# Attention and a maxout feed-forward net in one kernel: the last 64 queries of both heads as 64x64 matmul tiles

## The chip, the cores and the metric

The kernel runs on one core of a Trainium2 chip. The metric is the device time of one launch in microseconds; the profile's span, from the first to the last instruction, is a little shorter.

## The reference

Attention over 8 batches of 12 heads, 448 tokens and a head dimension of 64, with one extra term in the softmax's denominator, is followed by a three-way maxout feed-forward net over all 3584 tokens. Cut to its core:

```python
scores = scale * np.matmul(q, k.transpose(0, 1, 3, 2))
m = np.max(scores, axis=-1, keepdims=True)
e = np.exp(scores - m)
attn = e / (np.sum(e, axis=-1, keepdims=True) + np.exp(-m) + 1e-09)
attn_out = np.matmul(attn, v)
x = attn_out.transpose(0, 2, 1, 3).reshape(B * S, H * D)      # 3584 x 768
h = np.maximum(np.maximum(x @ w1, x @ w2), x @ w3)            # 768 x 768 each
out = h @ w_out                                               # 768 x 768, float32
```

## The kernel before

**Groups and pairs.** The 96 heads are worked in 24 groups (`NI`) of four heads, three groups to a batch; a group has two pairs (`pr`) of two heads (`hh`). Inputs are cast to float16 by the loading DMAs. K and Q are brought to head-dimension-first form, for the later groups by DMA transposes on SP's queue (`transpose_dma`), and GpSimd copies shifted halves of Q (`shift_q`).

**Scores.** `scores` computes transposed scores, so keys lie on partitions. The 448 keys of a head are seven blocks of 64, and a 128-partition tile holds two of them. Three such tiles hold six blocks of one head (`X1`, `X3`, `X2`); the seventh blocks of both heads of a pair share one (`TL`). A unit is two such tiles side by side in the two banks of one PSUM tile `stp`, made by four 64x64 matmuls, each in its own quarter of the array; ScalarE's exponential (L320) writes it to `e`.

**Weighted sums.** `av_tail` and `av_main` multiply `e` by V into a two-bank PSUM tile `avp`, one bank per head. V has a 65th column of constants, whose sum is the denominator. The 448 queries are cut into windows `w` of 128, so the fourth (`w` = 3) has only 64 real queries, and its other 64 weight columns are whatever lies next to them in `e`. `av_tail` covers the shared seventh blocks: for each window and head two 64x64x65 matmuls (L340), four to a window. `av_main` covers the other six blocks: for each head and window three 128x128x65 matmuls (L357). VectorE then makes the reciprocal of the denominators in `rb` (L367, L370) and writes the scaled sums to `xn` (L373).

**To the feed-forward net.** From group 6 on, a DMA transpose on SP's queue (`x_transpose_dma`, L423) brings `xn` to `xT`. The net's work for a batch is a list of pieces: 18 up pieces of six 128x128x448 matmuls (L440, PSUM tile `p_i`; VectorE takes the maximum into `hT`, L449 and L451), and 6 or 8 out pieces of six matmuls of 384 columns (L464, `op_ps`; VectorE scales them to `o_sb`, L471; SP's queue stores them, L481).

**PSUM.** The pool `ps_s` has three two-bank buffers, used in turn by `stp` and `avp`; `ps_b` has two one-bank buffers, used in turn by `p_i` and `op_ps`.

**Order.** It is written out by hand. From group 3 on each group has three visits, numbered `n` = 3i + vi. A visit issues the scores of two, two and three units, then in the first two visits `av` for one pair of the group before, and then pieces: `share(n)` gives the visit its part of the columns of work left, and `fill` pops pieces until a running `credit` is used up. The batch that is next is added by `add_batch` at the visits in `adds`. After the last visit come both `av` of group 23, its `x_transpose_dma`, what pieces are left, and the last batch.

Of the kernel before, what the change touches and what calls it, by code (L numbers as in the profile page):

```python
# [10 lines left out]
FP32 = mybir.dt.float32  # L11
FP16 = mybir.dt.float16
AF = mybir.ActivationFunctionType
ALU = mybir.AluOpType
ts = bass.ts

MMDT = FP16
LAMBDA = 256.0
# [3 lines left out]
def kernel(  # L22
# [11 lines left out]
    nc = tc.nc  # L34

    B, H, S, D = q.shape
# [5 lines left out]
    NP = GH // 2  # L42
    NG = H // GH
    NI = B * NG
    P = 128
    HP = 64
# [3 lines left out]
    D1 = D + 1  # L50
    XW = 512
    scale = 1.0 / math.sqrt(D)
# [3 lines left out]
    PE_QK = 7  # L56
    NF = 3
    PE_X = 2
    NEB = 2
    NV = 3  # L60

    cpool = ctx.enter_context(tc.tile_pool(name="const", bufs=1))
    att_pool = ctx.enter_context(tc.tile_pool(name="att", bufs=3))
    small = ctx.enter_context(tc.tile_pool(name="small", bufs=3))
    xn_pool = ctx.enter_context(tc.tile_pool(name="xn", bufs=3))
    xt_pool = ctx.enter_context(tc.tile_pool(name="xt", bufs=3))
    ht_pool = ctx.enter_context(tc.tile_pool(name="ht", bufs=2))
    out_pool = ctx.enter_context(tc.tile_pool(name="outp", bufs=6))
# [64 lines left out]
    first = {}  # L133
    for nm, src, eng in (("k", k, nc.sync), ("q", q, nc.scalar)):
# [7 lines left out]
            name=nc.get_next_instruction_name(),  # L142
# [13 lines left out]

    e_buf = [cpool.tile([P, NB * S + HP], MMDT, name=f"e{j}") for j in range(NEB)]
    v_buf = [cpool.tile([P, GH, 3, D + 2], MMDT, name=f"vx{j}") for j in range(NV)]
    vt_buf = [cpool.tile([P, NP, D + 2], MMDT, name=f"vt{j}") for j in range(NV)]
    for j in range(NV):  # L160
        nc.vector.memset(v_buf[j][:, :, :, D : D + 2], 1.0 / LAMBDA)
        nc.vector.memset(vt_buf[j][:, :, D : D + 2], 1.0 / LAMBDA)
    for j in range(NEB):
        nc.vector.memset(e_buf[j][:, NB * S : NB * S + HP], 0.0)
        blk = e_buf[j][:, 0 : NB * S].rearrange("p (n s) -> p n s", s=2 * S)
        nc.vector.memset(blk[:, :, NO : NO + HP], 0.0)

    def warm(n, cols=512):
        ps = ps_b.tile([128, 512], FP32, tag="b", name="warm")
# [104 lines left out]
    X1, X2, X3, TL = (0, 4), (2, 6), (1, 5), (3, 3)  # L274
# [9 lines left out]
    where = {(pr, hh, x): n for n, (pr, hh, x) in enumerate(blocks)}  # L284
# [37 lines left out]
    def e_col(n, w):  # L322

        return n * S + ((192, 320, 0, 128) if n % 2 == 0 else (0, 128, 256, 384))[w]

    xT = {}
    xn = {}
    avs = {}

    def av_tail(i, ej, pr, ws=(0, 1, 2, 3)):  # L330

        eF, vt = e_buf[ej], vt_buf[i % NV]
        ps = ps_s.tile([128, 2, 512], FP32, tag="s", name="avp")
        avs[i, pr] = ps
        n = where[pr, None, TL]
        for j, w in enumerate(ws):
            for hh in range(2):
                for half in range(2):
                    o = e_col(n, w) + half * HP
                    nc.tensor.matmul(  # L340
                        out=ps[half * HP : half * HP + HP, hh, j * D1 : (j + 1) * D1],
                        lhsT=eF[hh * HP : hh * HP + HP, o : o + HP],
                        rhs=vt[hh * HP : hh * HP + HP, pr, 0:D1],
                        start=(j == 0),
                        stop=False,
                        skip_group_check=True,
                    )

    def av_main(i, ej, pr, ws=(0, 1, 2, 3)):
        eF, vx = e_buf[ej], v_buf[i % NV]  # L350
        ps = avs.pop((i, pr))
        nw = len(ws)
        for hh in range(2):
            for j, w in enumerate(ws):
                for c, x in enumerate((X1, X3, X2)):
                    o = e_col(where[pr, hh, x], w)
                    nc.tensor.matmul(  # L357
                        out=ps[:, hh, j * D1 : (j + 1) * D1],
                        lhsT=eF[:, o : o + 128],
                        rhs=vx[:, 2 * pr + hh, (x[0]), 0:D1],  # L360
                        start=False,
                        stop=(c == 2),
                        skip_group_check=True,
                    )
        acc = ps[:, :, 0 : nw * D1].rearrange("p h (j d) -> p h j d", d=D1)
        rb = small.tile([P, 2, 4], FP32, tag="rb", name="rb")
        nc.vector.tensor_scalar(  # L367
            out=rb[:, :, 0:nw], in0=acc[:, :, :, D], scalar1=1.0 / LAMBDA, scalar2=None, op0=ALU.add
        )
        nc.vector.reciprocal(out=rb[:, :, 0:nw], in_=rb[:, :, 0:nw])  # L370
        if i not in xn:
            xn[i] = xn_pool.tile([P, NP, 4, 2, D], MMDT, tag="xn", name="xn")
        nc.vector.tensor_tensor(  # L373
            out=xn[i][:, pr, ws[0] : ws[0] + nw].rearrange("p j h d -> p h j d"),
            in0=acc[:, :, :, 0:D],
            in1=rb[:, :, 0:nw].unsqueeze(3).to_broadcast([P, 2, nw, D]),
            op=ALU.mult,
        )

    def prep_v(i, eng):  # L380
        t = raw[i]["v"]
        vx, vt = v_buf[i % NV], vt_buf[i % NV]
        eng.tensor_copy(out=vx[:, :, :, 0:D], in_=t[:, :, 1:4, :])  # L383
        t2 = t.rearrange("p (r h) t d -> p r h t d", r=NP)
        eng.tensor_copy(out=vt[0:HP, :, 0:D], in_=t2[0:HP, :, 0, 4, :])
        eng.tensor_copy(out=vt[HP:P, :, 0:D], in_=t2[HP:P, :, 1, 0, :])
# [34 lines left out]
    def x_transpose_dma(i):  # L421
        b, g = groups[i]
        nc.sync.dma_start_transpose(  # L423
            out=xt_tile(b)[:, 2 * g : 2 * g + 2, :].rearrange("p a (j s) -> p (a j) s", s=128),
            in_=xn[i].rearrange("p a j h d -> p (a j h d)"),
        )
# [61 lines left out]
    pieces = []  # L488
# [20 lines left out]
    credit = [0.0]  # L509

    def fill(cols):
        credit[0] += cols
        while pieces and credit[0] > 0:
            f, a, w = pieces.pop(0)
            f(*a)
            credit[0] -= w
        if not pieces:
            credit[0] = min(credit[0], 0.0)

    def left():  # L520
        return sum(w for _, _, w in pieces)

# [3 lines left out]
    STEP = 2 * NDC * (NO + 6)  # L526

    def av(i, ej, pr, part):
        av_tail(i, ej, pr, PW[part])
        av_main(i, ej, pr, PW[part])  # L530

# [6 lines left out]
    def attend(part, g, *steps):  # L538

        ej = (g + (part == "E") * NG) % NEB  # L540
        for st in steps:
# [3 lines left out]
            else:  # L545
                pg, pr = st[1:]
                av(pg, pg % NEB, pr, "O")

# [52 lines left out]
    visits = ((0, 1), (2, 3), (4, 5, 6))  # L601
    adds = {3 * (3 * b + 4) + (b >= PE_X): b for b in range(1, B - 1)}

    AVC = 2200

    def share(n):


        nxt = min([a for a in adds if a > n], default=3 * NI + 2)
        rest = range(n, nxt)  # L610
        sums = [AVC if m % 3 < 2 and m < 3 * NI else 0 for m in rest]
        return max(0, (left() + sum(sums)) / len(rest) - sums[0])
# [7 lines left out]
    for i in range(3, NI):  # L620
        ej, pj = (i + 1) % NEB, i % NEB
        first = i == 3
        if PE_QK <= i + 2 < NI:
            transpose_dma(i + 2)
        if first:
            load_v(i + 2)
        for vi, units in enumerate(visits):
            n = 3 * i + vi
            scores(i, ej, units)
            if i == 4 and vi == 0:  # L630
                prep_v(i, DV)
            if vi < 2:
                av(i - 1, pj, vi, "E" if first else "EO")
            if vi == 1 and i > 3 * PE_X:
                x_transpose_dma(i - 1)
            if n in adds:
                add_batch(adds[n])
            per = STEP if first and vi < 2 else share(n)
            if vi == 0 and first:
                x_transpose_pe(1, "E")  # L640
            if vi == 2 and first:
                x_transpose_pe(i - 1, "E")
                fill(per / 2)
                prep_v(i, DV)
                for w, cols in ((0, (0, NE)), (1, (0, NE)), (2, (NE, NO)), (2, (0, NE))):
                    add_up(0, *cols, [(w, f) for f in (0, 2, 4)])
                add_out(0)
                per = share(n)
            if vi == 2 and 3 < i <= 3 * PE_X:
                x_transpose_all(i - 1)  # L650
            if first:
                fill(per)
                per = 0
            if i + 1 < PE_QK and vi < 2:
                transpose_once(i + 1, "qk"[vi], (AC, DV)[vi])
            fill(per)
        if i + 1 < PE_QK:
            shift_q(i + 1, nc.gpsimd)
        if first:
            load_qk(i + 3)  # L660
        if i < 5:
            load_more(i + 3, i + 4)
        if 5 <= i + 1 < NI:
            prep_v(i + 1, nc.gpsimd)
        if PE_QK <= i + 2 < NI:
            shift_q(i + 2, nc.gpsimd)
        if i >= 5:
            load_more(i + 3, i + 4)

    av(NI - 1, NI % NEB, 0, "EO")  # L670
    av(NI - 1, NI % NEB, 1, "EO")
    x_transpose_dma(NI - 1)
    fill(float("inf"))
    add_batch(B - 1)
# [31 lines left out]
```

The softmax here doesn't subtract the row's maximum and nothing guards it: scores larger than these inputs give would overflow.

## Time and profile before

| | |
|---|---|
| median of 8 runs | 341.21 us (340.9 to 342.44) |
| the profiled execution: time / span | 341.24 us / 339.5 us |
| PE busy | 329.8 us, 97% |
| DVE busy | 189.3 us, 56% |
| ACT busy | 151.0 us, 44% |
| POOL busy | 146.7 us, 43% |
| mean granted TensorE clock | 0.996 |

The busy shares come from one profiled execution. A busy PE counts overlapping matmuls once, so matmuls are best priced by the distance between their starts. A group's row gives the line, the engine, the operation, what is written and read, the shapes, the count, the busy time, the mean of one, and the idle time of the engine before it with what ended it. A timeline's row gives the start, the time from the first start to the last end, the engine and what ran, merged over equal neighbours.

### The profile page before, as it was taken

How to read it: one execution, taken by the hardware profiler on the slowest of the kernel's cores; microseconds unless marked ns; L12 is line 12 of the kernel's file. 1: busy time of each engine (PE TensorE's matmuls, PEld its weight loads, DVE VectorE, ACT ScalarE, POOL GpSimd, SP SyncE). 2: the span in 40 equal slices, each digit the busy share in tenths (PEclk: the TensorE clock that was granted, in tenths of full speed). 3: DMA queues.
4: the chain of work that ended last, by engine and by line, in shares of the span. 5: the costliest groups of instructions: out<-in, count | busy, mean ns of one | idle time of the engine just before them, and what ended most of it. 6: DMA issues, size and time to landing. Idle time of an engine off the chain costs nothing.

```text
span 339.5 us, 9812 instructions
## 1 busy us (share of the span) xinstructions
PE 329.8 (97%) x4172; PEld 199.5 (59%) x4172; DVE 189.3 (56%) x410; ACT 151.0 (44%) x181; POOL 146.7 (43%) x260
## 2 busy tenths in 40 slices
PE   7899999999999999999999999999999999999994
PEld 4668788855555655555555655555555655555552
DVE  4556665565546555555545555546456556465552
ACT  3868856654554545453543445463543454200000
POOL 8686677971836077154547071936252000000000
PEclk9999999999999999999999999999999999999998
DMA  8999999699996997979996999999970440133006
GB/s 148 201 208 209 202 203 181 112 169 210 125 147 70 234 209 99 134 100 227 160 128 80 198 205 113 147 144 196 149 118 21 116 115 3 33 77 95 0 21 165
DMA packets 84812, 46.42 MB, mean 137 GB/s; under 512 B 53280, under 2 KB 81312, under 8 KB 84768
## 3 DMA queue, kind: packets, MB, share of 16 engines
q0 software_dynamic: 29120, 21.80, 47.1%
q1 hardware_dynamic: 55264, 23.60, 36.8%
q8 instruction: 32, 0.52, 0.6%
q10 hardware_dynamic: 384, 0.39, 0.4%
q14 instruction: 12, 0.10, 0.1%
HBM read 44.04 MB, written 11.01 MB: 162 GB/s over the span
## 4 chain that ended last, share of the span: by engine, by line
PE 93%; DVE 3%; ACT 2%; issue 1%; ACTq 0%
PE p_i L440 48%; PE op_ps L464 16%; PE stp L300 12%; PE avp L357 11%; PE avp L340 2%; ACT e L320 2%; PE warm L171 1%; DVE xn L373 1%; DVE QT L186 1%; PE trT L225 1%; ACT QT L184 1%; PE trT L209 1%; PE xtp L413 0%; DVE rb L370 0%; PE xtp L400 0%
## 5 line engine op out<-in xcount | busy, mean ns | idle before, releaser
L320 ACT ACTIVATE e<-stp 128x896 f16<-128x896 f32 (+4 forms) x171 | 144.2, 903 | 137.0 <-PE stp L300 136.6
L440 PE MATMUL p_i<-xT,w 128*128 128x448 f16 (+2 forms) x972 | 173.4, 332 | 0.2
L440 PEld LDWEIGHTS <-w 128*128 128x128 f16 x972 | 90.0, 98 | 68.2 <-issue 5.4
L245 POOL COPY QT<-QT 64x384 f16<-64x384 f16 (+1 forms) x84 | 47.1, 561 | 95.0 <-DMA QT<-ld_q 82.8
L451 DVE TENSOR_TENSOR hT<-hT,p_i 128x448 f16<-128x448 f16 (+2 forms) x96 | 59.7, 621 | 43.0 <-PE p_i L440 42.8
L464 PE MATMUL op_ps<-w,hT 128*128 128x384 f16 (+2 forms) x342 | 58.1, 323 | 0.0
L300 PE MATMUL stp<-QT,KT 64*64 64x448 f16 (+2 forms) x756 | 48.3, 338 | 2.3 <-ACT e L320 0.9
L464 PEld LDWEIGHTS <-hT 128*128 128x128 f16 x342 | 32.1, 98 | 23.0 <-issue 2.0
L357 PE MATMUL avp<-vx,e 128*128 128x65 f16 x1152 | 45.4, 193 | 0.0
L471 DVE TENSOR_SCALAR o_sb<-op_ps 128x384 f32<-128x384 f32 (+2 forms) x57 | 31.3, 550 | 23.7 <-PE op_ps L464 23.1
L449 DVE CAST hT<-p_i 128x448 f16<-128x448 f32 (+2 forms) x48 | 30.0, 625 | 23.9 <-PE p_i L440 23.8
L357 PEld LDWEIGHTS <-e 128*128 128x128 f16 x1152 | 38.8, 97 | 2.2
L373 DVE TENSOR_TENSOR xn<-avp,rb 128x512 f16<-128x512 f32 (+1 forms) x54 | 34.1, 632 | 1.9
L300 PEld LDWEIGHTS <-KT 64*64 64x64 f16 x756 | 16.0, 105 | 27.1 <-issue 24.2
L367 DVE TENSOR_SCALAR rb<-avp 128x8 f32<-128x8 f32 (+1 forms) x54 | 8.9, 166 | 40.0 <-PE avp L357 39.9
L383 POOL COPY vx<-ld_v 128x768 f16<-128x768 f16 x21 | 17.2, 819 | 7.3 <-issue 4.7
L340 PEld LDWEIGHTS <-e 64*64 64x64 f16 x768 | 14.8, 107 | 7.9 <-issue 1.4
L102 POOL DMA_DIRECT2D ld_k<-in_k_dram x24 | 17.2, 717 | 2.4 <-DMA w<-in_moe_w_out_dram 1.1
L102 POOL DMA_DIRECT2D ld_q<-in_q_dram x24 | 17.2, 716 | 2.1 <-DMA w<-in_moe_w_dram 1.1
L340 PE MATMUL avp<-vt,e 64*64 64x65 f16 x768 | 15.4, 192 | 0.6 <-ACT e L320 0.4
L115 POOL DMA_DIRECT2D ld_v<-in_v_dram x24 | 15.1, 628 | 2.0 <-DMA w<-in_moe_w_dram 1.2
L112 POOL DMA_DIRECT2D ld_v<-in_v_dram x24 | 15.2, 632 | 1.1 <-DMA w<-in_moe_w_dram 1.1
(43 smaller groups left out, 88.0 us busy)
## 6 DMA issues: line engine op xcount, KB each, us to landing
out_dram<-o_sb SPq DMA_DIRECT2D x54, 192.0 KB, 3.7
ld_v<-in_v_dram POOLq DMA_DIRECT2D x48, 128.0 KB, 4.7
ld_k<-in_k_dram POOLq DMA_DIRECT2D x23, 224.0 KB, 6.6
ld_q<-in_q_dram POOLq DMA_DIRECT2D x23, 224.0 KB, 7.3
w<-in_moe_w_dram POOLq DMA_DIRECT2D x9, 384.0 KB, 9.5
w<-in_moe_w_out_dram POOLq DMA_DIRECT2D x3, 384.0 KB, 8.5
xT<-xn SPq DMA_TRANSPOSE x18, 4.9
QT<-ld_q SPq DMA_TRANSPOSE x17, 5.2
```

Source lines behind the costliest of these rows:

```text
L102: nc.gpsimd.dma_start(out=tiles[nm][:, 1 : NP * T + 1].rearrange("x (r t) d -> x r (t d)", r=NP)[:, p0:p1], in_=src[:, p0:p1],)
L245: eng.tensor_copy(out=t[d0 : d0 + HP, o * 128 : (o + n) * 128], in_=t[s0 : s0 + HP, a * 128 : (a + n) * 128],)
L300: nc.tensor.matmul(out=stp[half * HP : half * HP + HP, par, j * qn : (j + 1) * qn], lhsT=k_block(i, pr, h2, x[half]), rhs=q_cols(i, pr, h2 ...
L320: nc.scalar.activation(out=dst, in_=src, func=AF.Exp, scale=scale)
L340: nc.tensor.matmul(out=ps[half * HP : half * HP + HP, hh, j * D1 : (j + 1) * D1], lhsT=eF[hh * HP : hh * HP + HP, o : o + HP], rhs=vt[hh * ...
L357: nc.tensor.matmul(out=ps[:, hh, j * D1 : (j + 1) * D1], lhsT=eF[:, o : o + 128], rhs=vx[:, 2 * pr + hh, (x[0]), 0:D1], start=False, stop= ...
L373: nc.vector.tensor_tensor(out=xn[i][:, pr, ws[0] : ws[0] + nw].rearrange("p j h d -> p h j d"), in0=acc[:, :, :, 0:D], in1=rb[:, :, 0:nw]. ...
L440: nc.tensor.matmul(out=p_i[:, j * qn : (j + 1) * qn], lhsT=w_sb[i][:, dc, ts(fc, 128)], rhs=xT[b][:, dc, q0 : q0 + qn], start=(dc == 0), s ...
L449: nc.vector.tensor_copy(out=dst, in_=src)
L451: nc.vector.tensor_tensor(out=dst, in0=dst, in1=src, op=ALU.max)
L464: nc.tensor.matmul(out=op_ps[:, 0:w], lhsT=hT[bp][:, fc, ts(t, 128)], rhs=wout_sb[:, fc, c : c + w], start=(fc == 0), stop=(fc == NFC - 1),)
L471: nc.vector.tensor_scalar(out=o_sb[:, c : c + w], in0=op_ps[:, 0:w], scalar1=1.0 / LAMBDA, scalar2=None, op0=ALU.mult,)
```

## The change

For the groups from 6 on (`LAST`), 36 pairs in all, `av` treats the first three windows as before, and the last window in a new function `av_last`:

- Its part of `av_tail` shrinks from four 64x64 matmuls to two, one per head.
- Its part of `av_main`, six 128x128 matmuls (three per head), becomes twelve 64x64 matmuls: for each of the three blocks of keys, the lower and the upper 64 keys (`r`) of both heads (`hh`). Head `hh` goes to output partitions 64·hh onwards, and the key half `r` to bank `r`.
- So the sum of the last window lies in two halves, in two banks. ScalarE copies one half to SBUF (`end`), and the function returned, `finish`, adds the other half to it on VectorE, makes the reciprocal there (`rl`), and lets ScalarE write the scaled rows of both heads to `xn`.
- `finish` is called after `one`, which issues one more piece of the feed-forward net (it raises the credit just above zero). `x_transpose_dma` moves behind `finish`. After the last visit the same happens for each of the two pairs.
- `xn` becomes three fixed buffers in place of a pool of three; the part that the last window no longer writes is zeroed once at the start by three VectorE memsets.

```diff
+    LAST = 6
-    xn_pool = ctx.enter_context(tc.tile_pool(name="xn", bufs=3))
...
+    xn_buf = [cpool.tile([P, NP, 4, 2, D], MMDT, name=f"xn{j}") for j in range(NV)]
+    for j in range(NV):
+        nc.vector.memset(xn_buf[j][HP:P, :, 3], 0.0)
...
+    def av_last(i, ej, pr):
+        eF, vx, vt = e_buf[ej], v_buf[i % NV], vt_buf[i % NV]
+        ps = avs[i, pr]
+
+        def tile_mm(r, hh, o, rhs, stop):
+            nc.tensor.matmul(
+                out=ps[hh * HP : hh * HP + HP, r, 3 * D1 : 4 * D1],
+                lhsT=eF[r * HP : r * HP + HP, o : o + HP],
+                rhs=rhs,
+                start=False,
+                stop=stop,
+                skip_group_check=True,
+            )
+
+        n = where[pr, None, TL]
+        for hh in range(2):
+            tile_mm(hh, hh, e_col(n, 3), vt[hh * HP : hh * HP + HP, pr, 0:D1], False)
+        for c, x in enumerate((X1, X3, X2)):
+            for r in range(2):
+                for hh in range(2):
+                    o = e_col(where[pr, hh, x], 3)
+                    rhs = vx[r * HP : r * HP + HP, 2 * pr + hh, x[0], 0:D1]
+                    tile_mm(r, hh, o, rhs, c == 2)
+
-    def av_main(i, ej, pr, ws=(0, 1, 2, 3)):
+    def av_main(i, ej, pr, ws=(0, 1, 2, 3), last=False):
...
+        if not last:
+            return None
+        end = small.tile([P, D1], FP32, tag="end", name="end")
+        rl = small.tile([P, 1], FP32, tag="rl", name="rl")
+        nc.scalar.activation(out=end, in_=ps[:, 1, 3 * D1 : 4 * D1], func=AF.Copy)
+
+        def finish():
+            nc.vector.tensor_tensor(out=end, in0=ps[:, 0, 3 * D1 : 4 * D1], in1=end, op=ALU.add)
+            nc.vector.tensor_scalar(
+                out=rl, in0=end[:, D:], scalar1=1.0 / LAMBDA, scalar2=None, op0=ALU.add
+            )
+            nc.vector.reciprocal(out=rl, in_=rl)
+            for hh in range(2):
+                h = slice(hh * HP, hh * HP + HP)
+                nc.scalar.activation(
+                    out=xn[i][0:HP, pr, 3, hh], in_=end[h, 0:D], func=AF.Copy, scale=rl[h]
+                )
+
+        return finish
...
+    def one():
+        if pieces:
+            fill(max(0.0, 1.0 - credit[0]))
...
     def av(i, ej, pr, part):
+        if i >= LAST:
+            av_tail(i, ej, pr, (0, 1, 2))
+            av_last(i, ej, pr)
+            return av_main(i, ej, pr, (0, 1, 2), True)
...
+            finish = None
             if vi < 2:
-                av(i - 1, pj, vi, "E" if first else "EO")
-            if vi == 1 and i > 3 * PE_X:
-                x_transpose_dma(i - 1)
+                finish = av(i - 1, pj, vi, "E" if first else "EO")
             if n in adds:
                 add_batch(adds[n])
             per = STEP if first and vi < 2 else share(n)
+            if finish:
+                one()
+                finish()
+            if vi == 1 and i > 3 * PE_X:
+                x_transpose_dma(i - 1)
...
-    av(NI - 1, NI % NEB, 0, "EO")
-    av(NI - 1, NI % NEB, 1, "EO")
+    for pr in range(NP):
+        finish = av(NI - 1, NI % NEB, pr, "EO")
+        one()
+        finish()
     x_transpose_dma(NI - 1)
```

More of the change, by code (lines that the diff above doesn't have):

```diff
@@ L365, in av_main @@
         acc = ps[:, :, 0 : nw * D1].rearrange("p h (j d) -> p h j d", d=D1)
-        rb = small.tile([P, 2, 4], FP32, tag="rb", name="rb")
+        rb = small.tile([P, 2, nw], FP32, tag=f"rb{nw}", name="rb")
         nc.vector.tensor_scalar(
-            out=rb[:, :, 0:nw], in0=acc[:, :, :, D], scalar1=1.0 / LAMBDA, scalar2=None, op0=ALU.add
+            out=rb, in0=acc[:, :, :, D], scalar1=1.0 / LAMBDA, scalar2=None, op0=ALU.add
         )
-        nc.vector.reciprocal(out=rb[:, :, 0:nw], in_=rb[:, :, 0:nw])
+        nc.vector.reciprocal(out=rb, in_=rb)
         if i not in xn:
-            xn[i] = xn_pool.tile([P, NP, 4, 2, D], MMDT, tag="xn", name="xn")
+            xn[i] = xn_buf[i % NV]
         nc.vector.tensor_tensor(
@@ L375, in av_main @@
             in0=acc[:, :, :, 0:D],
-            in1=rb[:, :, 0:nw].unsqueeze(3).to_broadcast([P, 2, nw, D]),
+            in1=rb.unsqueeze(3).to_broadcast([P, 2, nw, D]),
             op=ALU.mult,
         )
+        if not last:
[15 more added lines that the diff above has]
+        return finish
     def prep_v(i, eng):
```

## The prediction

> **What bounds the kernel now.** I read the page's shares and its chain of work first, then the windows, the groups, and the timeline of one visit and of the end.
>
> ```profile
> PE 329.8 (97%) x4172; PEld 199.5 (59%) x4172; DVE 189.3 (56%) x410; ACT 151.0 (44%) x181; POOL 146.7 (43%) x260
> PE 93%; DVE 3%; ACT 2%; issue 1%; ACTq 0%
> ```
>
> ```profile
> 55.00:295.00 240.00, 239.85 (x3024) 139.12 (x3017) 133.62 (x270) 114.53 (x134) 105.62 (x191) 1.00 0.88 136
> ```
>
> The windows' row (PE, PEld, DVE, ACT, POOL busy, then the clock) covers the stage in which nearly all of the changed work lies: PE has 0.15 us idle in 240 at full clock. TensorE sets the time there, so what its stream loses is gained, unless a new wait opens a hole. The groups and the timeline of one visit price that stream:
>
> ```profile
> L357 PE MATMUL avp<-vx,e 128*128 128x65 f16 x1152 | 45.4, 193 | 0.0
> L340 PE MATMUL avp<-vt,e 64*64 64x65 f16 x768 | 15.4, 192 | 0.6 <-ACT e L320 0.4
> ```
>
> ```profile
> 32.66 0.23 PE L340 MATMUL avp<-vt,e 64*64 64x65 f16 x8
> 32.82 0.55 PE L357 MATMUL avp<-vx,e 128*128 128x65 f16 x12
> ...
> 203.19 0.57 PE L300 MATMUL stp<-QT,KT 64*64 64x448 f16 x8
> 203.59 0.29 PE L340 MATMUL avp<-vt,e 64*64 64x65 f16 x16
> 203.68 1.73 ACT L320 ACTIVATE e<-stp 128x896 f16<-128x896 f32 x2 [1.67 <-PE stp L300]
> 203.82 0.92 PE L357 MATMUL avp<-vx,e 128*128 128x65 f16 x24
> 204.58 2.43 PE L440 MATMUL p_i<-xT,w 128*128 128x448 f16 x12
> 204.78 0.17 DVE L367 TENSOR_SCALAR rb<-avp 128x8 f32<-128x8 f32 x1 [0.86 <-PE avp L357]
> 204.98 0.20 DVE L370 RECIPROCAL rb<-rb 128x8 f32<-128x8 f32 x1
> 205.22 0.69 DVE L373 TENSOR_TENSOR xn<-avp,rb 128x512 f16<-128x512 f32 x1
> 205.91 0.63 DVE L449 CAST hT<-p_i 128x448 f16<-128x448 f32 x1
> ```
>
> The reader should see that a run of 12 full matmuls takes 0.55 us and one of 24 takes 0.92, so one more costs 0.37/12 = 31 ns; from start to start, 203.82 to 204.58, it is 0.76/24 = 31.7 ns. Eight more quarter-array matmuls cost 0.29 - 0.23 = 0.06 us, or 7.5 ns each (8.75 by the starts: 0.23 against 0.16 to the next kind). Four quarters therefore cost 30 to 35 ns, as much as one full matmul.
>
> **The change on TensorE.** For one pair it removes six full matmuls, 6 x 31.7 = 190 ns. It adds twelve quarters in three sets of four, each set filling all four quarters of the array: 3 x 30 to 3 x 35 = 90 to 105 ns. Of the tail's last four quarters two go. The two that stay must still precede the first set in their own quarters of the array, so I count nothing saved; at best it is 2 x 7.5 = 15 ns. The array changes between 64- and 128-wide tiles as often as before, since `av_last` stands between the tail and the main part. Saved per pair: 85 to 115 ns, and I take 95, from the middle of the quarters' rows. Over 36 pairs that is 3.4 us (3.1 to 4.1).
>
> One rule speaks against the change. The Trainium skill, TensorEngine Tiling (Array Packing), "Instruction Overhead", gives each matmul about 60 cycles and warns against tiling a dimension that is already small. At the 2.4 GHz of TensorE: Matmul & The Clock Gate that is, as an estimate, 25 ns; ten more matmuls would then cost 250 ns against 190 and lose 2.2 us in all. The 16 quarters within 0.29 us do not show this floor.
>
> **The change on VectorE.** The scaling shrinks from 512 columns to 384; between the groups' 424 ns at 256 and 691 at 512 that is about 558, a gain of 133 ns. `finish` adds a sum of 65 columns (the same line gives about 225 ns), a one-column add (167 at eight columns, 161 at four) and a reciprocal (203 and 179): with gaps of 35 ns some 0.67 us. Net it is +0.5 us per pair, 19 us in all, and VectorE goes from 189 to about 208 us. It has 44% idle, so its load alone costs nothing. The three memsets at the start lie in its wait of 1.9 us for the first K and cost nothing; without that cover they would be some 0.3 us (112 ns for the 128x64 one).
>
> **The change on ScalarE.** A copy of 65 columns and two scalings of 64: the rows of 384 and 512 columns (505 and 592 ns) give 0.68 ns a column and leave 245 ns at zero, those of 512 and 1024 (592 and 1024) leave about 160, so one costs between 0.21 and 0.29 us. I take 0.25, hence 0.75 per pair and 27 us in all: 151 to 178, still well under the span.
>
> **The new waits.** The copy stands behind this visit's exponentials on ScalarE. `finish` on VectorE stands behind the eviction of `one`'s piece, and the two scalings, waiting for it, stand ahead of the next visit's exponentials. Take the tightest visit, with out pieces, from its first score at T. The sums end at T+1.30, the scaling starts at 1.5 and ends at 2.5, the exponentials end at 2.25 and the copy at 2.5 to 2.8; the piece's eviction ends at 3.06, the added sum at 3.3, the reciprocal at 3.7, the scalings at 4.2. Who waits? The next `avp` needs its buffer at 3.7 or later (two pieces of 0.97 us, then scores) and gets it at 3.3, 0.4 us early. The third piece needs the first one's PSUM buffer at 3.24 and gets it at 3.06. The next exponentials start up to 0.4 us late, but their `stp` buffers are needed again only one visit (3.3 us or more) after their scores. So nothing reaches TensorE, though with margins of 0.2 to 0.4 us; I allow 0.2 us in all, up to 2. `one` changes when pieces are issued, not which: by the credit rule five visits get two out pieces in place of three. SP's `x_transpose_dma` moves about 2 us later, past the stores of that piece; its `xT` is read three visits later. The exception is the last one:
>
> ```profile
> 296.83 0.93 PE L357 MATMUL avp<-vx,e 128*128 128x65 f16 x24
> 297.60 2.43 PE L440 MATMUL p_i<-xT,w 128*128 128x448 f16 x12
> 299.87 6.09 PE L464 MATMUL op_ps<-w,hT 128*128 128x384 f16 x36
> 305.79 20.59 PE L440 MATMUL p_i<-xT,w 128*128 128x448 f16 x108
> ```
>
> **The end.** Before, two up and six out pieces follow the last sums, the transpose is issued at 298.95 and lands 2.7 us later (301.68 in the trace), 4.1 us before it is needed. By the credit rule one up piece fewer is left; the other goes between the two pairs and one out piece ahead of the last `finish`. From the last sums VectorE works off the scaling, that piece, and `finish`, and ScalarE's scalings end 3.2 us later; plus 2.7 that is 5.9 us, against 5.9 us of out pieces and up to 0.35 us in which these wait for VectorE's late evictions. So the cover is just used up. I take 0.2 us lost there; with the median landing of 4.9 us it would be 2.2.
>
> **The sum.** 36 x 0.095 = 3.4, less 0.2 for waits, less 0.2 at the end: 3.0 us off. The profiled execution's 341.24 us (339.5 of span, 1.74 around it, unchanged) becomes 338.2; it stands 0.03 above the median.
>
> **The rivals.**
> 1. New waits give back a large part. For it: the margins above are smaller than one piece's eviction (0.56 or 0.62 us), and VectorE's queue is in order. Against it: 44% of VectorE is idle. Ten to sixty ns a pair lost is 0.4 to 2.2 us, so 338.6 to 340.4.
> 2. The last transpose lands late: 2.2 us lost, 340.2. For it: the cover is spent. Against it: loads are over by then, and the last landing took 2.7.
> 3. Slower: the four quarters do not overlap in `av_last`, because here, unlike in the tail, each has a moving operand of its own and sets follow each other on the same sums. It decides from 190/3 = 63 ns a set. At the full pitch of 31.7 ns each, ten more matmuls cost 317 against 190 ns: +127 x 36 = 4.6 us, 345.8. Against it: the scores' L300 row starts eight quarter matmuls in 0.40 us at 448 columns, and full matmuls already sum onto the same columns at 31 ns.
> 4. No change: quarters at about 60 ns a set. No row has that pitch.
>
> **How the numbers follow.** The forecast, 337.2 to 338.9, has 0.66; the first rival 0.14, the second 0.07, the third (or waits that cost more than the saving) 0.10, no change 0.03. The range runs from 337.2 (4.1 us saved and nothing lost) to 340.4, the end of the first two rivals. This kernel's measurement can tell about 0.2%, 0.7 us: the first three cases hold 0.87, of which I move 0.04 to within it (the far end of the first two rivals) and 0.02 to slower (waits beyond them): faster by more 0.81, within it 0.07, slower by more 0.12.
>
> **What the profile after would show.** From the first quarter matmul (L340 and the new line) to the first piece about 0.90 us in place of 0.99; sets of four about 31 ns apart; PE still without idle between 55 and 290 us; VectorE near 208 us and ScalarE near 178. I would be wrong if idle time of PE ended by VectorE or ScalarE appears in the visits, if sets take over 63 ns, or if the last batch's first up piece waits for `xT`.

## The result, and the profile after

The changed kernel takes 338.58 us (median of 11 runs, 337.88 to 340.63) against 341.15 (median of 32, 340.66 to 342.44): 2.57 us less, a ratio of 0.9933 with an interval of 0.9922 to 0.9945. Ratios weigh all runs but three that lie over 1.5% above the fastest of their kernel, two with the transpose later still and one with the quarters twice, so they differ a little from those of the medians. The forecast was 338.2 in 337.2 to 340.4. The profiled execution took 339.21 us, with a span of 337.3.

The page after, the shares and the chain first, then the groups of the last window (line numbers have moved: the main matmuls are now L388, the up pieces L490, the out pieces L514, the transpose of `xn` L473):

```profile
PE 326.3 (97%) x4316; PEld 195.5 (58%) x4316; DVE 199.7 (59%) x521; ACT 183.0 (54%) x289; POOL 146.6 (43%) x260
...
PE 85%; DMA 6%; DVE 3%; ACT 2%; issue 1%; POOL 0%; ACTq 0%; POOLq 0%
...
L424 ACT ACTIVATE xn<-end,rl 64x64 f16<-64x64 f32 x72 | 24.9, 346 | 34.7 <-DVE rl L421 34.2
...
L388 PE MATMUL avp<-vx,e 128*128 128x65 f16 x936 | 38.6, 194 | 0.0
```

The 216 full matmuls are gone (1152 to 936). New in the chain is a DMA, with 6% of the span; the chain counts such a transfer in full, and TensorE lost far less to it (0.64 us, below). One visit, in the timeline (the first quarters of the last window stand in short rows of their own, left out here):

```profile
206.69 0.57 PE L304 MATMUL stp<-QT,KT 64*64 64x448 f16 x8
...
207.09 0.26 PE L344 MATMUL avp<-vt,e 64*64 64x65 f16 x12
...
207.22 0.26 PE L361 MATMUL avp<-vx,e 64*64 64x65 f16 x10
...
207.42 0.73 PE L388 MATMUL avp<-vx,e 128*128 128x65 f16 x18
...
207.99 3.19 PE L490 MATMUL p_i<-xT,w 128*128 128x448 f16 x16
...
209.29 0.23 ACT L414 ACTIVATE end<-avp 128x65 f32<-128x65 f32 x1 [0.44 <-PE p_i L490]
209.32 0.62 DVE L499 CAST hT<-p_i 128x448 f16<-128x448 f32 x1 [0.15 <-PE p_i L490]
...
209.87 0.22 DVE L417 TENSOR_TENSOR end<-avp,end 128x65 f32<-128x65 f32 x1
...
210.50 0.70 ACT L424 ACTIVATE xn<-end,rl 64x64 f16<-64x64 f32 x2 [0.99 <-DVE rl L421]
```

From the first quarter matmul to the first piece it is 207.09 to 207.99, 0.90 us, against 0.99 before. All quarters together take 0.33 (0.23 before, so the net ten more cost 0.10), the full ones 0.57 (0.76 before). Over all such visits of the two traces the medians are 990 and 899 ns: 91 ns a pair. `finish` runs beside the pieces, and the up matmuls go on.

But one piece did wait. In the timeline (SP's issue of the third group's transpose, then the first up piece of its batch):

```profile
110.31 1.78 SPq L473 DMA_TRANSPOSE xT<-xn  x1
...
117.70 0.92 PE L490 MATMUL p_i<-xT,w 128*128 128x448 f16 x4
118.87 0.92 PE L490 MATMUL p_i<-xT,w 128*128 128x448 f16 x4 [0.25 <-DMA xT<-xn]
```

The batch starts with four matmuls, which need only the first two groups; the fifth waits until that transpose has landed, at 118.83, 8.5 us after its issue. Beyond the usual distance of two starts (0.19 us) that is 0.41 us lost, and a second batch loses 0.23. Waits of TensorE are counted in this way from here on. The windows show it: 49.75 us busy of 50, where before all stages from 100 us on were full (first the row before, then the row after).

```profile
100.00:150.00 50.00, 50.00 (x627) 28.30 (x625) 27.67 (x56) 23.94 (x28) 24.68 (x44) 1.00 0.97 142
```

```profile
100.00:150.00 50.00, 49.75 (x662) 27.97 (x660) 30.08 (x81) 32.19 (x54) 27.50 (x49) 1.00 1.07 152
```

### The profile page after: what moved, and what is told of

Same layout as the page of the kernel before. It is cut to its first block, busy times and chain, and to the rows that moved or that the text cites. A ratio compares the mean times of both kernels' runs of the same rounds, so it can differ in the third digit from the quotient of the medians.

```text
span 337.3 us, 10248 instructions
## 1 busy us (share of the span) xinstructions
PE 326.3 (97%) x4316; PEld 195.5 (58%) x4316; DVE 199.7 (59%) x521; ACT 183.0 (54%) x289; POOL 146.6 (43%) x260
## 4 chain that ended last, share of the span: by engine, by line
PE 85%; DMA 6%; DVE 3%; ACT 2%; issue 1%; POOL 0%; ACTq 0%; POOLq 0%
PE p_i L490 48%; PE op_ps L514 13%; PE stp L304 10%; PE avp L388 9%; DMA xT<-xn 5%; ACT e L324 2%; PE avp L344 1%; DMA ld_q<-in_q_dram 1%; PE avp L361 1%; DVE xn L404 1%; DVE QT L190 1%; PE trT L229 1%; PE xtp L463 0%; ACT QT L188 0%; PE trT L213 0%
## 5 line engine op out<-in xcount | busy, mean ns | idle before, releaser
L490 PE MATMUL p_i<-xT,w 128*128 128x448 f16 (+2 forms) x972 | 173.2, 332 | 0.5 <-DMA xT<-xn 0.2
L490 PEld LDWEIGHTS <-w 128*128 128x128 f16 x972 | 90.2, 98 | 69.3 <-issue 6.3
L514 PE MATMUL op_ps<-w,hT 128*128 128x384 f16 (+2 forms) x342 | 58.5, 323 | 0.0
L514 PEld LDWEIGHTS <-hT 128*128 128x128 f16 x342 | 32.0, 98 | 22.4 <-issue 2.0
L424 ACT ACTIVATE xn<-end,rl 64x64 f16<-64x64 f32 x72 | 24.9, 346 | 34.7 <-DVE rl L421 34.2
L388 PE MATMUL avp<-vx,e 128*128 128x65 f16 x936 | 38.6, 194 | 0.0
L388 PEld LDWEIGHTS <-e 128*128 128x128 f16 x936 | 32.0, 97 | 2.3
L398 DVE TENSOR_SCALAR rb<-avp 128x6 f32<-128x6 f32 (+2 forms) x54 | 8.8, 164 | 36.8 <-PE avp L388 36.8
L404 DVE TENSOR_TENSOR xn<-avp,rb 128x384 f16<-128x384 f32 (+2 forms) x54 | 29.3, 543 | 1.8
L344 PEld LDWEIGHTS <-e 64*64 64x64 f16 x624 | 13.7, 107 | 8.2 <-issue 1.8
L414 ACT ACTIVATE end<-avp 128x65 f32<-128x65 f32 x36 | 8.2, 227 | 17.1 <-PE p_i L490 12.4
L115 POOL DMA_DIRECT2D ld_v<-in_v_dram x24 | 15.0, 627 | 1.9 <-DMA w<-in_moe_w_dram 1.2
```

The lines of the kernel that those rows point to most:

```text
L388: nc.tensor.matmul(out=ps[:, hh, j * D1 : (j + 1) * D1], lhsT=eF[:, o : o + 128], rhs=vx[:, 2 * pr + hh, (x[0]), 0:D1], start=False, stop= ...
L404: nc.vector.tensor_tensor(out=xn[i][:, pr, ws[0] : ws[0] + nw].rearrange("p j h d -> p h j d"), in0=acc[:, :, :, 0:D], in1=rb.unsqueeze(3) ...
L424: nc.scalar.activation(out=xn[i][0:HP, pr, 3, hh], in_=end[h, 0:D], func=AF.Copy, scale=rl[h])
L490: nc.tensor.matmul(out=p_i[:, j * qn : (j + 1) * qn], lhsT=w_sb[i][:, dc, ts(fc, 128)], rhs=xT[b][:, dc, q0 : q0 + qn], start=(dc == 0), s ...
L514: nc.tensor.matmul(out=op_ps[:, 0:w], lhsT=hT[bp][:, fc, ts(t, 128)], rhs=wout_sb[:, fc, c : c + w], start=(fc == 0), stop=(fc == NFC - 1),)
```

## The experiments

Two theories for the gap between 36 x 91 ns = 3.3 us and the 2.57 measured stood at the start: T, waits for late transposes, and C, many short waits for VectorE and ScalarE. Times in brackets are the lowest and highest run; ratios are to the kernel before in the same job (341.25 to 341.31 us).

**The changed kernel again.**

> The changed kernel once more, as the mark for the others beside it. Both theories: about 338.6 us, 2.5 us under the kernel before. The theory of the late transposes (T: the third group's transpose of a batch is issued some 2 us later and its batch starts some 2 us earlier, so TensorE waits for xT in some batches, by a different amount in each execution) expects runs that scatter by 1 us or more, between 337.9 and 340.6. The theory of the chain of waits (C: the 0.7 us that are missing from 36 x 91 ns = 3.3 us are lost in short waits for VectorE and ScalarE in every visit) expects runs as close together as those of the kernel before.

339.56 us (338.25 to 342.75, 12 runs), ratio 0.996 (0.9933 to 0.9987). By the medians the gain is 1.75 us in this job, not the 2.5 that both theories expected. The scatter of 4.5 us, against about 1.2 for the kernel before in the same job, is T's. This profiled execution took 342.27 us, and its timeline of TensorE and two of its windows show where the most went:

```profile
117.39 0.92 PE L490 MATMUL p_i<-xT,w 128*128 128x448 f16 x4
120.78 4.49 PE L490 MATMUL p_i<-xT,w 128*128 128x448 f16 x14 [2.47 <-DMA xT<-xn]
```

```profile
117.50:121.00 3.50, 1.03 (x8) 0.41 (x5) 0.91 (x3) 1.37 (x3) 0.00 (x0) 1.00 1.59 311
121.00:124.20 3.20, 3.20 (x10) 1.28 (x9) 1.55 (x5) 0.69 (x2) 0.66 (x2) 0.51 0.81 168
```

The transpose took 9.5 us, TensorE lost 2.64 us, and then the granted clock was 0.51 for 3.2 us: eight matmuls started 373 ns apart in place of 189, which is 1.5 us more. One late landing cost 4.1 us.

**Pacing as before.**

```diff
             if finish:
+                ahead = credit[0]
                 one()
+                per -= max(0.0, 1.0 - ahead)
                 finish()
```

> The piece that is issued ahead of finish is taken out of the visit's own share, so the pieces are paced as before the change. By the credit rule the time from the issue of the third group's transpose to the batch's first up piece grows from 7.4 to 8.4 us to about 8.8 to 9.6. T expects most of the waits for xT gone: 338.0 us (337.8 to 338.3) and less scatter. C expects no change, 338.6, since finish and its waits stay.

338.67 us (338.35 to 338.79, 4 runs), ratio 0.9922 (0.991 to 0.9935); no wait for `xT` in its trace. It was run once more beside later kernels:

> The paced kernel once more beside the two above, to be compared on the same chip: 338.7 us, runs within 0.5 us of each other.

338.86 us (337.89 to 339.36, 6 runs), ratio 0.9925 (0.9908 to 0.9941), again with no wait for `xT` in the trace. The long runs are gone, as T says, but six runs spread over 1.5 us, as those of the kernel before in that job, and not over 0.5 as expected. Both medians lie 0.4 us or more above T's 337.8 to 338.3, so something else is missing too.

The times of the five batches, read from the traces (from the issue of the third group's transpose to the batch's first up piece / to its landing, us; four matmuls, 0.76 us, precede the first use):

| kernel | batch 2 | 3 | 4 | 5 | 6 |
|---|---|---|---|---|---|
| before | 11.4 / 7.0 | 10.5 / 6.6 | 11.4 / 8.1 | 10.5 / 6.1 | 11.4 / 2.7 |
| after | 7.4 / 8.5 | 7.4 / 6.0 | 8.4 / 7.4 | 7.4 / 8.3 | 8.4 / 4.7 |
| after again | 6.1 / 9.5 | 7.4 / 5.6 | 8.4 / 3.2 | 7.4 / 3.8 | 8.4 / 4.4 |
| paced | 9.3 / 3.0 | 8.5 / 4.1 | 9.5 / 5.6 | 8.5 / 6.0 | 9.4 / 3.0 |
| paced again | 9.3 / 9.6 | 8.5 / 3.0 | 9.3 / 7.0 | 8.5 / 5.2 | 9.3 / 3.0 |
| transpose later still | 5.5 / 9.3 | 7.4 / 4.1 | 6.7 / 3.3 | 7.4 / 3.8 | 7.4 / 4.4 |

In the second trace of the paced kernel the transpose of batch 2 took 9.6 us and landed 0.5 us before its first use: the pacing covers the landings seen for these five transposes, with little to spare.

**Batches one visit later.** `adds` has `+ 2 * (b >= PE_X)` in place of `+ (b >= PE_X)`, on top of the pacing.

> As the paced kernel, and each batch from the third on joins the list of pieces one visit later, which leaves about 13 us between the issue of the transpose and its first use, above the longest landing in the trace of before (9.3 us). T expects no wait for xT at all: 337.9 us (36 x 91 ns off 341.15), runs within 0.5 us. C expects 338.6.

338.59 us (338.08 to 339.81, 6 runs), ratio 0.9923 (0.9907 to 0.9939), no better than the paced kernel: T's 337.9 and its spread of 0.5 us are both missed. Its profiled execution (339.81) has no wait for `xT`, but one of 0.88 us in a run of out matmuls, put down to "issue"; the last section comes back to it.

**The tiles alone.** `av_main` returns before the copy, and the last loop calls neither `one` nor `finish`.

> The 64x64 tiles alone: ScalarE's copy, finish and the piece ahead of it are left out, so the last 64 queries' sums of the groups from 6 on never reach xn (its last window is zeroed once), and the transposes are issued where they were before. T and C both expect the whole of TensorE's saving, 36 x 91 ns = 3.3 us: 337.9 us, with little scatter, since the transposes have their old 10 to 11 us.

338.67 us (338.39 to 338.99, 4 runs), ratio 0.9924 (0.9911 to 0.9937): the same as the paced kernel, which does everything. So the copy, `finish` and all their waits cost nothing that can be measured once the pieces are paced, and C falls. Yet this kernel too gains only 2.64 us. From the 200th score matmul (counted from 0) to the last matmul it takes 287.38 us, and the kernel before takes 290.66: the 3.28 us are there. The paced kernel takes 287.56 and 287.37 in its two traces. What is lost lies outside that stretch.

**The transpose later still.** `x_transpose_dma` moved behind the visit's `fill(per)`.

> The changed kernel with x_transpose_dma issued after the pieces of its visit, some 2 to 3 us later still. The theory of the late transposes (T) expects every late landing to become a wait: with about 5 us in place of 7.4 to 8.4 between issue and first use, and the landings of 4.7 to 9.4 us that the runs so far show for these five transposes, some 1 to 4 us of waiting in most of the five batches, 5 to 15 us in all (waits over 3 us cost more, as the granted clock falls after them): 344 to 354 us. The theory of many short waits for VectorE and ScalarE (C) expects no change, about 339.

342.98 us (338.96 to 344.22, 10 runs), ratio 1.0024 (0.9996 to 1.0051). The direction is T's and against C, and it is enough to undo the gain. The size was missed: the transpose moved by only 0 to 1.9 us (table), because `finish` had ended shortly before the visit did, and only batch 2 waited in the trace, 3.08 us. The expectation has the granted clock fall after waits over 3 us; after this one it stayed at 1.00 (a row for the wait, then one for the matmuls behind it):

```profile
117.50:121.29 3.79, 0.87 (x8) 0.34 (x5) 0.91 (x3) 1.43 (x3) 0.00 (x0) 1.00 1.27 175
121.29:124.10 2.81, 2.81 (x18) 1.33 (x21) 1.69 (x5) 0.70 (x2) 0.89 (x2) 1.00 1.16 283
```

That execution took 341.13 us. The six runs over 342.8 us have a mean granted clock of 0.990 to 0.994, the four others 0.997 to 0.999, so in those six a fall of the clock may well have added to the wait; none of them has a trace.

**A load of instructions moved.** `warm(24, 170)` in place of `warm(8)`, on the paced kernel.

> The paced kernel with its first warming run cut finer, 24 matmuls of 170 columns in place of 8 of 512: the same columns, 16 more pairs of instructions on TensorE. In the traces with the 64x64 tiles a 16 KB load of instructions starts 0.44 us before the last matmul, the third last store takes 0.91 to 0.99 us to issue in place of 0.53, and the span ends 5.5 to 5.9 us after the last matmul starts in place of 5.25. If that load is the cause (theory L), it now starts some 2.6 us earlier, the store issues in about 0.5 us again, and the time falls by 0.3 us against the paced kernel, to about 338.3. If the longer end has another cause, nothing changes, 338.7.

338.65 us (338.43 to 339.37, 6 runs), ratio 0.9924 (0.9909 to 0.9939). The load moved from 0.44 to 2.4 us before the last matmul, and the third last store issued in 0.53 us again. But the next stores landed later (the second of SP's last three 3.6 us after its issue, 2.4 in the kernel before), and the end stayed at 5.77 us. So the slow issue was not the cause; whether the load is, this shift was too small to tell.

**No piece ahead of `finish`.**

> The changed kernel with finish called at once, without a piece issued ahead of it. Pacing is that of before and the transposes are issued earlier, so T alone expects 338.0. But VectorE then stands at the added sum until ScalarE's copy is done (2.5 to 2.8 us after the visit's first score) and evicts the first piece some 1 us later than now; a visit with three pieces has its third one wait 0.5 to 0.8 us for that PSUM buffer. With about 20 such visits that is 10 us: 345 to 350 us, with idle time of TensorE before the third piece. If the piece ahead covers nothing, 338 to 339.

352.18 us (351.89 to 352.24, 4 runs), ratio 1.0317 (1.0301 to 1.0332). The timeline of one visit:

```profile
121.01 0.23 ACT L414 ACTIVATE end<-avp 128x65 f32<-128x65 f32 x1 [0.44 <-PE p_i L490]
121.27 0.23 DVE L417 TENSOR_TENSOR end<-avp,end 128x65 f32<-128x65 f32 x1 [0.37 <-ACT end L414]
...
121.80 0.60 DVE L499 CAST hT<-p_i 128x448 f16<-128x448 f32 x1
...
122.45 0.92 PE L490 MATMUL p_i<-xT,w 128*128 128x448 f16 x4 [0.31 <-DVE hT L499]
```

VectorE waits for the copy, evicts the first piece late, and the third piece waits for its buffer. Such a wait stands in 22 places of the trace, 0.45 to 0.80 us each, and one of 1.3 us at the end: 14 us. The one piece ahead is what makes the change worth having.

**Scalings on VectorE.** On the paced kernel, `tensor_scalar` in place of the two activations in `finish`.

> The paced kernel with the two last scalings on VectorE in place of ScalarE. They took 346 ns each on ScalarE; on VectorE I expect about 0.15 us each, so the transpose is issued some 0.4 us earlier and ScalarE is 25 us less busy. T expects 338.6 (the paced kernel has hardly any wait for xT left); if what is missing were waits for ScalarE, 338.2 or less; if VectorE's load were the limit, over 339.

340.17 us (339.47 to 341.05, 12 runs), ratio 0.9967 (0.9956 to 0.9978): 1.5 us worse than the paced kernel. A scaling took 252 ns by the median on VectorE, not 150; VectorE went to 220.7 us, and TensorE waited for its evictions, 0.24 to 0.40 us in five places of the trace.

**The kernel before again.**

> The kernel before, for a second trace of it. In the one trace so far the span ends 5.25 us after the last matmul starts; with the 64x64 tiles it is 5.5 to 5.9 us in eight traces. If the change lengthens the end, this trace has 5.25 again; if the end scatters by itself, it may lie anywhere from 5.2 to 5.9. From the 200th score matmul to the last matmul both expect 290.7 us as in the first trace.

341.39 us, 290.66 us from the 200th score matmul to the last matmul, and 5.12 from there to the end. So both traces of the kernel before end early. Of the twelve traces with the 64x64 tiles ten take 5.49 to 5.88, the tiles alone among them (5.64), so the copy and `finish` are not needed for it; the two kernels that follow here take 5.21 and 5.00. The end is longer with the change in most traces, not in all; the last section comes back to it.

**The quarters twice.** The loop over `X1, X3, X2` runs twice, on the paced kernel.

> The paced kernel with the twelve 64x64 matmuls of av_last issued twice (the sums of the last 64 queries of the groups from 6 on are doubled, denominators too): three more sets of four per pair. If TensorE's stream sets the time and a set costs 31 ns, 36 x 3 x 31 ns = 3.3 us more than the paced kernel's 338.67: 342.0. If the quarters did not overlap, 36 x 12 x 31 ns = 13 us more; if something else set the time, less than 1 us more.

344.69 us (342.48 to 349.35, 6 runs), ratio 1.0089 (1.006 to 1.0118). The head of a pair, from the first quarter to the first full matmul, grew from 324 to 432 ns by the medians: 36 ns a set, 3.9 us in all, near the first expectation. The rest is not in the sets but in waits of TensorE such as this one, amid matmuls whose operands had long been there:

```profile
117.53 0.33 PE L388 MATMUL avp<-vx,e 128*128 128x65 f16 x5
...
119.23 0.58 PE L388 MATMUL avp<-vx,e 128*128 128x65 f16 x13 [1.37 <-issue]
```

**From group 3 on.** `LAST = 3`, on the paced kernel.

> The paced kernel with the new last window from group 3 on in place of group 6: six more pairs, 6 x 91 ns = 0.55 us off the paced kernel if the short visits of groups 4 to 6, of one or two pieces, still cover finish: 338.1. If they do not, waits of 0.3 to 0.8 us in up to six visits eat it up: 338.5 to 341.

340.49 us (339.76 to 343.85, 8 runs), ratio 0.9985 (0.996 to 1.001). The short visits do not cover `finish`: up to 75 us TensorE waits for VectorE's evictions, for `avp`'s buffer and, in the three transposes on TensorE, 0.41 us each for ScalarE's scaling.

## Why the prediction was right, and where a step failed

**TensorE.** Right: 91 ns a pair against 95, 3.28 us in the stretch against 3.4. The sets of four start 31 to 36 ns apart, and three more of them cost 36 ns each with the quarters twice, where the floor of 25 ns per matmul that spoke against the change would make it 100; it does not hold for matmuls in different quarters of the array. The quarters twice also show that the stream sets the time.

**The waits in the visits.** Right: in the changed kernel TensorE waits in its visits for nothing but `xT`, and in the paced kernel for nothing. The visit with out pieces that starts at 113.06 us in the trace of after keeps the worked times within 0.15 us: the eviction of the piece ends 3.03 us after the first score (3.06 was worked out), the added sum at 3.17 (3.3), the scalings at 4.29 (4.2). The piece ahead was rightly seen as part of the cover, and its worth is now known: 352.18 against 338.6.

**VectorE and ScalarE.** VectorE rose by 10 us, not 19. The three new rows are 218, 154 and 164 ns, and the gaps of 35 ns had been counted as busy; that leaves 14.5 us of instructions, and the busy time counts neighbours that overlap once. ScalarE rose by 32, not 27, since a scaling took 346 ns and not 250; the copy took 227. The Trainium skill, ScalarE: Activation LUTs, "What ACT_TABLE_LOAD costs", says that each per-partition pointer operand adds about 93 ns; these two rows of nearly equal width differ by 119 (they also differ in partitions and in where they read). Neither error touched the time.

**The end.** The sum was right, and the loss it allowed did not come. The transpose was issued at 300.35 and landed at 303.39, 0.2 us after the last batch's first piece began, but the first four matmuls of a batch (0.76 us) do not need it, and the piece ran on. The prediction had not counted these four, neither here nor where it put the cover before at 4.1 us; it was 4.9. In the timeline of after:

```profile
296.75 0.74 PE L388 MATMUL avp<-vx,e 128*128 128x65 f16 x18
297.33 6.01 PE L514 MATMUL op_ps<-w,hT 128*128 128x384 f16 x36
299.62 0.70 ACT L424 ACTIVATE xn<-end,rl 64x64 f16<-64x64 f32 x2 [0.74 <-DVE rl L421]
303.18 5.08 PE L490 MATMUL p_i<-xT,w 128*128 128x448 f16 x26
```

**The step that failed** is the sentence on SP's queue: the transpose moves about 2 us later, "its `xT` is read three visits later", and "`one` changes when pieces are issued, not which". Both halves were true and neither was priced. A transpose issued 2 us later meets a batch started about 2 us sooner, because `one` runs the pieces of the old batch out early: 10.5 to 11.4 us became 7.4 to 8.4, while the row of before already had landings up to 9.3. The rival of a late transpose was put at the last batch alone, where none was lost.

**A term that was missing:** the end of the span, from 5.1 or 5.25 us after the last matmul to 5.5 to 5.9 in most traces, for a cause that stays open. With the transposes the books close for the profiled executions: 3.28 saved, 0.64 lost to the two waits, 0.50 at the end, 0.12 more before the 200th score matmul (no more than the two traces of before differ by there), is 2.0 us; the spans differ by 2.1.

**Luck.** That the time came so near the forecast is in part luck. The saving was sized well, but the two allowances of 0.2 us met nothing, and what was lost in the profiled execution, 0.64 and 0.50 us, stood nowhere in the sum. The execution that was profiled in the second job lost 4.1 us to one landing and took 342.27 us, outside the range.

The paced kernel is the best complete version that was run: 338.67 and 338.86 us in its two jobs, without the long runs of the changed one. Its median is not below the 338.58 us of the first job, and it is not shown to be faster in its best executions.

## What to carry to other kernels

When a step moves, work out the time from each transfer's issue to its first use before and after, and hold it against the longest landing in the traces, not the median (2.7 to 9.3 us about a median of 4.9 in the trace of before); something that issues work ahead shortens that time from the other side. A helper that runs ahead should pay back what it took from the schedule's budget. On a saturated TensorE, four 64x64 matmuls in the four quarters cost about what one full matmul costs here (31 to 36 ns against 31.7), and the gain was had in full in the visits where each new step behind it had work in front of it; from group 3 on, where the visits are short, it was lost.

## What the runs showed of the hardware that was not expected

**A wait of 2.6 us slowed the clock, one of 3.1 us did not.** After a wait of TensorE of 2.64 us the granted clock fell to 0.51 for about 3 us. After one of 3.08 us, at the same place in another trace, it stayed at 1.00 and the matmuls started 189 ns apart as usual; after the waits of 0.23 and 0.41 us it stayed too. So the length of the wait alone does not decide it here, and what does is not shown.

**Loads of instructions reach the end of the kernel.** The trace has packets of 16 KB in an instruction queue, 32 in the kernel before and 34 after. The Trainium skill, Runtime: NRT & Kernel Launch, "Instruction fetch mechanics", says that each engine's instructions come in blocks of 16 KiB, 256 instructions; TensorE has 288 more here, in line with the two more loads. Where the last load begins sorts the ends: in ten traces it begins 0.25 to 2.4 us before the last matmul, and the span ends 5.49 to 5.88 us after it; in four (both of before, the quarters twice, from group 3 on) it begins 5.2 us or more before, and the end is 5.00 to 5.25. That is an association in the traces; the one experiment on it moved the load too little to isolate it.

**TensorE may run out of instructions.** Three waits put down to "issue" amid matmuls (0.88 us in the kernel with its batches one visit later, 1.53 and 1.03 with the quarters twice) each ended 1.36 to 1.42 us after a 16 KB load of instructions had. That points to instructions that came late; no experiment isolates it.
